# A longer hold on the first weights and x rows loaded by SyncE: a fused attention and gated-MLP kernel

## The chip, the cores and the metric

The kernel runs on one core of one Trainium2 chip. The time is device microseconds (us) of that core; "span" is the same execution as the profiler saw it, some 1.7 us shorter. A profile shows five engines: TensorE (PE for matmuls, PEld for weight loads), VectorE (DVE), ScalarE (ACT), GpSimd (POOL) and SyncE (SP), and the DMA queues: q1 is fed by SyncE, q10 by ScalarE, q0 by GpSimd. "L302" is line 302 of the kernel.

## The reference

```python
# x: 2048 x 640; wq: 640 x 6144; wo: 6144 x 640; 32 heads of 192, the last 512 cached keys and values
xn = layernorm(x)
q  = xn @ wq                                        # 32 heads
p  = softmax(q @ k[-512:].T * 192 ** -0.5)          # per head
s  = concat(p @ v[-512:]) @ wo
g  = silu((sigmoid(xn @ w_gate) * (xn @ w_up)) @ w_down)
return x + s * g
```

All inputs and the output are bf16.

## The kernel before

It starts with the gated MLP (stage B) and then does attention in 8 groups of 4 heads; each group has 4 units of 512 queries, so `NG = 8`, `NB = 4` and 32 units. The parts that matter:

The start. VectorE fills a corner of the first gate weights with zeros. Nothing needs the zeros: ScalarE's load of these weights writes over them, so it must wait for the fill, and this holds the load back by a chosen time.

```python
nc.vector.memset(wg_sb[:, 0, 0:2 * P], 0.0)       # P = 128; the hold
load_x(0, 1)                                      # SyncE: x tile 0, 160 KB
load_x(1, 1)                                      # SyncE: x tile 1
load_f(nc.scalar, wg_sb, wg_r, 0, 4, 0, 3)        # ScalarE: first gate weights, 384 KB
load_f(nc.sync, wg_sb, wg_r, 0, 4, 3, NCD)        # SyncE: the other chunks of them, 256 KB
load_f(nc.sync, wu_sb, wu_r, 0, 4, 0, 3)
load_x(2, 1)
# ... more weights and x on SyncE ...
dummy(17)                                         # matmuls on zeros while the data come
# ... statistics and centring of x tiles 0 and 1 ...
turn_pe(0, 0, 1)                                  # transposes of x tile 0 on TensorE
turn_pe(0, 1, 3, 2)
tile_half(0, 0, 0, 0, 0, 1)                       # the first real matmul, L302; needs the 384 KB
```

The end of a unit. `project` multiplies a tile of 128 queries with `wo` and adds it to `acc`; in the last group but one (`g == NG - 2`) GpSimd then applies the gate and adds the row of x, so that the last group only has to multiply, add and store.

```python
def project(u, q, k, out_eng=None, add=nc.vector, two=True):
    ...                                           # matmuls, L527
    else:
        nc.vector.tensor_tensor(cols(acc[:, t, :]), res, cols(acc[:, t, :]), ALU.add)   # L542
    if g == NG - 2:
        x_sb = fin.tile([P, D], BF16, name="row")                 # two buffers
        nc.gpsimd.dma_start(x_sb[:], xf[t * P:(t + 1) * P, :])    # L545
        nc.gpsimd.tensor_tensor(acc[:, t, :], acc[:, t, :], gate[:, t, :], ALU.mult)    # L546
        nc.gpsimd.tensor_tensor(acc[:, t, :], acc[:, t, :], x_sb[:], ALU.add)           # L547
    yield
```

In the last group VectorE multiplies the projection with the gate (L508, `o_sb`, which frees the PSUM bank) and adds `acc` (L513).

The softmax here doesn't subtract the row's maximum and nothing guards it: scores larger than these inputs give would overflow.

## Time and profile before

| | before |
|---|---|
| time, median of the 4 runs beside the changed kernel | 922.30 us (922.08 to 923.22) |
| span of the profiled run | 920.7 us |
| TensorE busy | 99% |
| first weights issued, landed, first real matmul | 1.17, 5.70, 5.74 us |
| x tile 1 landed | 4.88 us |
| GpSimd's last addition of a row ends | 885.5 us |

The prediction below shows the lines behind this table.

### The profile page before, as it was taken

The page shows a single profiled execution, that of the slowest core. Times are in us where ns is not written, and L with a number is a line of the kernel's source. Part 1 is how long each engine was busy: PE and PEld are TensorE (multiplying, and loading weights), DVE is VectorE, ACT ScalarE, POOL GpSimd, SP SyncE. Part 2 cuts the span into 40 slices and gives each one's busy share as a digit, 9 for nine tenths or more (in the row PEclk, how much of TensorE's full clock was granted, in tenths as well). Part 3 has the DMA queues.
Part 4 walks back from the last instruction along what each step waited for, and adds up shares of the span by engine and source line. Part 5 has one row for each costly group of instructions (what it writes and reads, how often), then busy time and mean ns, then how long its engine had stood idle before and what let it go on. Part 6 is the DMA issues. An engine that isn't in the chain of part 4 may idle for free.

```text
span 920.7 us, 24960 instructions
## 1 busy us (share of the span) xinstructions
PE 913.5 (99%) x11314; PEld 623.1 (68%) x11333; DVE 494.3 (54%) x987; ACT 302.9 (33%) x334; POOL 134.9 (15%) x163
## 2 busy tenths in 40 slices
PE   9999999999999999999999999999999999999998
PEld 4445455466868686867676777777776767676875
DVE  6552522544646464646555555545554646464677
ACT  4222222255142424242333333242424151515150
POOL 2000100001002000200020011001100111165733
PEclk9999999999999999999999999999999999999999
DMA  9830330125434333342425162516261615273535
GB/s 319 165 44 1 89 87 1 43 62 88 78 63 109 84 58 83 94 98 42 98 84 108 36 105 79 113 30 110 66 111 42 114 61 95 64 114 106 95 72 139
DMA packets 172106, 79.35 MB, mean 86 GB/s; under 512 B 149952, under 2 KB 167568, under 8 KB 172000
## 3 DMA queue, kind: packets, MB, share of 16 engines
q1 hardware_dynamic: 164640, 55.85, 31.5%
q0 software_dynamic: 5808, 20.52, 7.8%
q8 instruction: 88, 1.44, 0.7%
q10 hardware_dynamic: 1552, 1.39, 0.5%
q14 instruction: 18, 0.15, 0.1%
HBM read 39.45 MB, written 2.62 MB: 46 GB/s over the span
## 4 chain that ended last, share of the span: by engine, by line
PE 98%; DVE 1%; DMA 0%; issue 0%; ACT 0%; DVEq 0%
PE bank L527 22%; PE bank L456 21%; PE bank L478 19%; PE bank L438 18%; PE bank L260 8%; PE bank L272 6%; PE bank L302 3%; PE bank L404 1%; DMA wg_sb<-in_B_w_gate_dram 0%; PE bank L562 0%; DVE gate L513 0%; DVE o_sb L508 0%; ACT xnT L246 0%; PE bank L244 0%; DVEq L664 0%
## 5 line engine op out<-in xcount | busy, mean ns | idle before, releaser
L442 ACT ACTIVATE E<-bank 128x1024 bf16<-128x1024 f32 x256 | 255.3, 1022 | 457.0 <-PE bank L438 456.9
L456 PE MATMUL bank<-xnT,wq_sb 64*128 64x512 bf16 x1800 | 226.4, 376 | 0.0
L527 PE MATMUL bank<-wo_sb,oT 64*128 64x320 bf16 x2688 | 205.2, 296 | 0.0
L438 PE MATMUL bank<-qT,kT 64*128 64x512 bf16 x1536 | 200.7, 376 | 0.0
L478 PE MATMUL bank<-vbuf,E 64*128 64x193 bf16 x4096 | 195.3, 243 | 0.3 <-DVE o_sb L508 0.3
L478 PEld LDWEIGHTS <-E 64*128 64x128 bf16 x4096 | 178.8, 94 | 10.7 <-issue 1.1
L527 PEld LDWEIGHTS <-oT 64*128 64x128 bf16 (+1 forms) x2892 | 163.4, 94 | 30.6 <-issue 0.3
L463 DVE CAST qT<-bank 128x1024 bf16<-128x1024 f32 x90 | 110.2, 1225 | 128.5 <-PE bank L456 128.5
L456 PEld LDWEIGHTS <-wq_sb 64*128 64x128 bf16 x1800 | 106.2, 100 | 86.9 <-issue 0.4
L438 PEld LDWEIGHTS <-kT 64*128 64x128 bf16 x1536 | 88.2, 94 | 73.4
L491 DVE TENSOR_TENSOR o_st<-bank,rden 128x768 bf16<-128x768 f32 x128 | 122.6, 958 | 4.4
L542 DVE TENSOR_TENSOR acc<-bank,acc 128x640 f32<-128x640 f32 x96 | 79.1, 824 | 20.1 <-PE bank L527 20.1
L118 POOL DMA_DIRECT2D vbuf<-in_A_v_cache_dram x28 | 21.1, 753 | 310.5 <-PE bank L478 307.6
L461 DVE COPY seen<-bank 128x2 f32<-128x2 f32 x90 | 14.4, 160 | 79.1 <-PE bank L456 79.1
L490 DVE RECIPROCAL rden<-bank 128x4 f32<-128x4 f32 x128 | 23.4, 183 | 60.1 <-PE bank L478 59.0
L272 PE MATMUL bank<-wd_sb,hT 128*128 128x128 bf16 (+1 forms) x377 | 52.4, 298 | 0.4
L272 PEld LDWEIGHTS <-hT 128*128 128x128 bf16 x384 | 29.7, 98 | 23.1
L266 DVE TENSOR_TENSOR hT<-bank,sig 128x512 bf16<-128x512 f32 x36 | 24.8, 690 | 37.1 <-ACT sig L263 37.1
L260 PE MATMUL bank<-xnT,wu_sb 128*128 128x512 bf16 x177 | 44.6, 379 | 0.2
L260 PE MATMUL bank<-xnT,wg_sb 128*128 128x512 bf16 x176 | 44.5, 379 | 0.2
L263 ACT ACTIVATE sig<-bank 128x512 bf16<-128x512 f32 x36 | 21.5, 597 | 55.8 <-PE bank L260 52.7
L97 POOL DMA_DIRECT2D wq_sb<-in_A_wq_dram x7 | 6.3, 904 | 210.4 <-PE bank L456 210.4
(53 smaller groups left out, 408.5 us busy)
## 6 DMA issues: line engine op xcount, KB each, us to landing
wo_sb<-in_A_wo_dram SPq DMA_DIRECT2D x7, 960.0 KB, 5.6
wq_sb<-in_A_wq_dram POOLq DMA_DIRECT2D x7, 960.0 KB, 6.2
k_st<-in_A_k_cache_dram POOLq DMA_DIRECT2D x14, 384.0 KB, 5.4
vbuf<-in_A_v_cache_dram POOLq DMA_DIRECT2D x28, 192.0 KB, 3.3
row<-in_A_x_dram POOLq DMA_DIRECT2D x16, 160.0 KB, 3.1
oT<-o_st SPq DMA_TRANSPOSE x128, 3.5
x_sb<-in_A_x_dram SPq DMA_DIRECT2D x3, 640.0 KB, 9.5
wd_sb<-in_B_w_down_dram SPq DMA_DIRECT2D x1, 1920.0 KB, 13.7
```

Source lines behind the costliest of these rows:

```text
L260: nc.tensor.matmul(bank[k][:, half, 0:r1 - r0], lhsT=w[:, c, f * P:(f + 1) * P], rhs=xnT[:, b, c, r0:r1], start=(c == 0), stop=(c == NCD - 1))
L266: nc.vector.tensor_tensor(hT[b][:, f, r0:r1], bank[k][:, 1, 0:r1 - r0], sig[:, 0:r1 - r0], ALU.mult)
L272: nc.tensor.matmul(wide(k)[:, d0:d1], lhsT=hT[b][:, f, q * P:(q + 1) * P], rhs=wd_sb[:, f, d0:d1], start=(f == 0), stop=(f == NF - 1))
L302: nc.tensor.matmul(bank[k][:, half, :], lhsT=xcT[:, c, t * P:(t + 1) * P], rhs=w[:, c, fg * FT:(fg + 1) * FT], start=(c == 0), stop=(c == ...
L438: nc.tensor.matmul(bank[k][:, i, :], lhsT=kT[r, pr, j, c * P:(c + 1) * P], rhs=q[r, pr * DJ + j, :], start=(j == 0), stop=(j == DJ - 1))
L442: nc.scalar.activation(E[u, pr][:, c, :, :], bank[k][:], AF.Exp, scale=scale_qk)
L456: nc.tensor.matmul(bank[k][:, half, :], lhsT=wq[r, c, col:col + DJ * (P - 1) + 1:DJ], rhs=xnT[r, b, c, :], start=(c == 0 and not second), ...
L463: nc.vector.tensor_copy(qT[u][:, 2 * m:2 * m + 2, :], bank[k][:])
L478: nc.tensor.matmul(o4[:, q, 0:DH + 1], lhsT=e[r, c, h % 2, q * P:(q + 1) * P], rhs=vbuf[r, h, c, 0:DH + 1], start=(turn == 0 and qq == 0 a ...
L491: nc.vector.tensor_tensor(o_st[u][:, :, h * DH:(h + 1) * DH], o4[:, :, 0:DH], rden[:].to_broadcast([P, TQ, DH]), ALU.mult)
L527: nc.tensor.matmul(res[:, half, :], lhsT=oT[u][r, cc, q * P:(q + 1) * P], rhs=wo[r, cc, half * HD:(half + 1) * HD], start=(turn == 0 and c ...
L542: nc.vector.tensor_tensor(cols(acc[:, t, :]), res, cols(acc[:, t, :]), ALU.add)
```

## The change

Two intentions: to hold the first weights a little longer, so that x tile 1 passes ahead of them; and to take the row loads, with their issue and their wait, off GpSimd, and issue them before the projection that they belong to.

```diff
-        nc.vector.memset(wg_sb[:, 0, 0:2 * P], 0.0)
+        nc.vector.memset(wg_sb[:, 0:2, 0:3 * P], 0.0)
...
         res = bank[k][:, :, 0:HD]
+        if g == NG - 2:
+            x_sb = fin.tile([P, D], BF16, name="row")
+            nc.sync.dma_start(x_sb[:], xf[t * P:(t + 1) * P, :])
         for turn in range(2 if two else 1):
...
         if g == NG - 2:
-            x_sb = fin.tile([P, D], BF16, name="row")
-            nc.gpsimd.dma_start(x_sb[:], xf[t * P:(t + 1) * P, :])
             nc.gpsimd.tensor_tensor(acc[:, t, :], acc[:, t, :], gate[:, t, :], ALU.mult)
```

## The prediction

> **What bounds the kernel now.** I read the page first: busy shares, then the chain that ended last.
>
> ```profile
> PE 913.5 (99%) x11314; PEld 623.1 (68%) x11333; DVE 494.3 (54%) x987; ACT 302.9 (33%) x334; POOL 134.9 (15%) x163
> ...
> PE 98%; DVE 1%; DMA 0%; issue 0%; ACT 0%; DVEq 0%
> ```
>
> TensorE is 99% busy of a span of 920.7 us, and 98% of the chain that ended last is its matmuls; the granted clock stands in the top tenth in all 40 slices. A change that removes no matmul can win only the holes in TensorE's row. I looked for them as distances between matmul starts over 0.5 us: there are four in the whole run, before 5.74, 11.25, 14.01 and 882.88 us. The diff touches the first and the last. The first is in the chain of waits of the first 8 us (start, duration, what):
>
> ```profile
> 1.00 0.15 DVE wg_sb L172
> 1.15 0.02 issue
> 1.17 4.53 DMA wg_sb<-in_B_w_gate_dram
> 5.70 0.04 issue
> 5.74 0.38 PE bank L302
> ```
>
> The zero fill of the first gate weights (L172) releases the weights' load on ScalarE's queue; this 384 KB load lands 4.53 us after its issue, and the first real matmul follows at once. From there to the end TensorE's order is fixed and nearly gapless, so whatever moves this landing moves the end by as much. The last hole is in the chain around 880 us:
>
> ```profile
> 878.35 0.83 PE bank L527 x12
> ...
> 879.21 0.83 DVE o_sb L508
> ...
> 880.13 1.96 DVE gate L513
> 882.09 0.75 DVE o_sb L508
> 882.84 0.04 issue
> 882.88 0.84 PE bank L478 x16
> ```
>
> The matmul at 882.88 needs a PSUM bank that VectorE had still to empty (L508); VectorE was late because its addition L513 took 1.96 us where the same form takes 0.82 elsewhere. The matmuls on both sides of this hole start 0.666 us apart, against some 0.2 for an ordinary step: it costs about 0.45 us. What held VectorE is in GpSimd's timeline of that moment:
>
> ```profile
> 877.27 0.58 POOL L545 DMA_DIRECT2D row<-in_A_x_dram  x1
> 877.86 1.41 POOL L546 TENSOR_TENSOR acc<-acc,gate 128x640 f32<-128x640 f32 x1
> 880.02 1.39 POOL L547 TENSOR_TENSOR acc<-acc,row 128x640 f32<-128x640 f32 x1 [0.75 <-DMA row<-in_A_x_dram]
> 881.36 0.58 POOL L545 DMA_DIRECT2D row<-in_A_x_dram  x1
> ```
>
> GpSimd's addition of the x row runs from 880.02 to 881.41, over the start of VectorE's L513. The work belongs to group 6's tiles, whose projection ended near 870: GpSimd is more than 10 us behind, because it issues each row's load itself and then waits for it. The tile view of the row gives that price:
>
> ```profile
> L545 POOL DMA_DIRECT2D row<-in_A_x_dram x16: 549/577/590, 764.5 to 881.4; - x16
> L547 POOL TENSOR_TENSOR acc<-acc,row x16: 1390/1392/1394, 804.3 to 884.1; 128x640 f32<-128x640 f32 x16
> ...
>   DMA row<-in_A_x_dram: 19.7, 14
> ```
>
> **What the Trainium skill says.** "SBUF — State Buffer", section "Who interferes with whom": a VectorE operation with two SBUF inputs contends with a GpSimd operation that reads SBUF, and the second to start blocks until the first is done. L513 (o_sb plus acc, both in SBUF) beside L547 is this pair, and the trace agrees: 1.96 and 2.05 us in the two collisions against 0.82, each lasting until just after GpSimd's end. L508 and L542 read PSUM and one SBUF tile and keep their 0.82 us beside GpSimd work. "DMA: Bandwidth & Descriptors", section "Issuing engines are not separate DMA queues": another issuing engine saves only sequencer time. The trace agrees in part: an issue costs GpSimd 0.577 us and SyncE 0.33 to 0.45. "VectorE: DVE Perf Modes", section "Zero memsets can be issued as uint32": one cycle per element, bf16 zeros as half as many words. The trace shows 256 bf16 columns as 128 uint32 in 165 ns.
>
> **The change, part by part.**
>
> (1) Zero fill. 256 columns become 2 x 384 = 768, so 384 words for 128. Two fills in the trace (one word 60 ns, 128 words 165 ns) give 0.83 ns a word; the page's cycle at 0.96 GHz gives 1.04. Estimate: 256 more words, 0.21 to 0.27 us, and the weights' issue at about 1.40 for 1.17. VectorE itself next works at 3.04 and ScalarE at 4.21 after its table load, so only the landing counts. The DMA packets show why one would want it: nearly all of x tile 1 (issued 1.18) has moved by 3.45, but its last 3 of 128 packets go at 4.23 to 4.42, after the weights' packets began at 3.01; tile 1 lands at 4.88. With later weights these stragglers should go first and tile 1 land some half microsecond sooner. But TensorE never waits for tile 1: its transposes at 6.50 follow the matmul before them without a hole. And the weights? Most of their packets are through by 4.7; the tail to 5.28 seems to be the engine that was late with x. That engine has the same bytes to move either way, so the landing should shift by less than the delay. I take +0.05 us, between -0.2 and +0.27.
>
> (2) Row loads. GpSimd loses 16 issues of 0.577 us (9.2 us) and most of 19.7 us of waiting; SyncE gains 16 issues of about 0.4 us. Nothing of this is on TensorE's path but the collisions, so I worked through SyncE's order in the second pass over group 6 (845 to 868 us). There are two row buffers, so a load waits for the addition two tiles earlier; a GpSimd tile is 1.47 + 1.41 = 2.88 us, just under the 2.96 us at which TensorE delivers tiles (1.33 values plus 1.63 projection). Rows 0 to 3 go ahead of the four transposes issued from 857.77; these take some 1.3 us each, so row 4 is issued at about 863.0 and lands 2.3 to 2.7 us later (2.29 was the first x tile's time), near 865.5. Its addition starts then, and the seven operations from it through the last addition, back to back, end near 875.5, for 885.5 before. That is before the 880.13 collision, which goes: -0.45 us. But VectorE's first L513, at 874.28, met an idle GpSimd before and would now meet the last addition or the multiplication before it. Its slack: the bank it delays by way of the next L508 is ready at 875.85 and wanted at 876.71, 0.86 us. A block of up to 1.4 us at a phase I cannot fix costs 0 to 0.6 us; I take 0.2.
>
> Sum: 922.26 + 0.05 - 0.45 + 0.2 = about **922.05 us**, so 0.02% faster.
>
> **The rivals.**
> - SyncE becomes the wait. Head of line: in the first pass the rows stand behind eight key transposes (798.27 to 810.2), and the output transposes then stand behind rows that wait for GpSimd. My walk puts those of unit 26 7 us later, those of unit 27 12 us later and those of unit 29 1 us later. For: they were ready to go at 810.25, 822.37 and 869.40. Against: they are wanted at about 846, 857 and 896. It would need another 10 us.
> - The last values load, in GpSimd's order behind the row work, moves. It is issued at 839.30 and lands at 842.46; TensorE wants it at 845.22. I get an issue near 837, so more slack. Were rows to land 5 us late each time, it would become the bound and cost several us. Unlikely.
> - The weights land later by the whole delay, 0.27 us, or fall behind SyncE's next load of 256 KB, 0.75 us at the 340 GB/s seen there. The issue stays ahead of that one (1.40 against 1.65). Time: 922.3, or 922.8 in the worst case.
> - The transfers are hidden anyway and the collision only moves: 922.2 to 922.5.
> - Both parts win: weights land sooner for the missing contention and no collision is left: 921.6.
>
> **Range and chances.** All paths lie within 1.5 us of 922; 2% would be 18 us. The runs before spread over 0.25 us. I give 921.5 to 922.6. Faster by over 2% has 0.5%, slower by over 2% 0.5% (a wait on SyncE that I overlooked), the rest is the same.
>
> **What would show it.** In the profile after: no POOL L545; the zero fill at 0.37 to 0.44 us; x tile 1's statistics starting near 4.5 instead of 4.91; the first L302 matmul between 5.6 and 6.0. GpSimd's last L547 should end between 874 and 879 instead of 885.5. VectorE's eight full-width L513 should hold at most two long ones, among the first two, and none at 880; the 0.29 us of TensorE waiting for o_sb should be gone or sit before 877 to 878. The waits of L547 for the row should fall from 19.7 us to under 10. The prediction is wrong if TensorE shows a new wait on oT or vbuf (SyncE's order), if the first matmul starts after 6.1 (the weights lost more than their delay), or if GpSimd still works at 880.

## More of the kernel before

One more reading of the kernel before is needed for the comparison: TensorE's timeline just after the start. Its columns are start, duration, engine, line, operation, output and inputs, shapes and count.

```profile
7.41 1.25 PE L302 MATMUL bank<-wg_sb,xnT 128*128 128x512 bf16 x5
8.50 1.89 PE L302 MATMUL bank<-wu_sb,xnT 128*128 128x512 bf16 x8
```

Five matmuls of 512 columns begin at 7.41 and the next group at 8.50, so one takes 0.22 us (1.09 / 5). The duration of a group says less, because matmuls overlap.

## The result, and the profile after

| | before | after |
|---|---|---|
| time, median of 4 runs | 922.30 us (922.08 to 923.22) | 925.47 us (924.66 to 926.54) |
| span of the profiled run | 920.7 us | 924.8 us |
| first weights issued, landed | 1.17, 5.70 us | 1.44, 7.77 us |
| x tile 1 landed | 4.88 us | 3.58 us |
| GpSimd's last addition of a row ends | 885.5 us | 881.5 us |

The ratio is 1.0033 (95% interval 1.0016 to 1.0051): 0.3% slower, small but clear of noise, where 0.02% faster was predicted. Ratios here are the mean time of one kernel's fast runs over that of the other's of the same rounds, so not quite the ratio of the medians. The profiled run of the changed kernel is the slowest of its four, so its parts below add up to 4.1 us and not to the 3.2 us between the medians.

**The start.** The chain that ended last in the changed kernel, in order of time (start, duration, what):

```profile
1.02 0.39 DVE wg_sb L172
1.42 0.02 issue
1.44 6.34 DMA wg_sb<-in_B_w_gate_dram
7.77 0.04 issue
7.81 0.58 PE bank L302
```

The fill takes 0.39 us, as predicted, and the load goes out at 1.44. But the load now takes 6.34 us for 4.53, and the first real matmul starts at 7.81: 2.07 us later, for 0.27 us of hold. And the matmuls that follow are slow. The changed kernel's timeline of TensorE, the groups that answer to the two shown of before (and the first one, for the wait in brackets):

```profile
7.81 0.58 PE L302 MATMUL bank<-wg_sb,xnT 128*128 128x512 bf16 x1 [2.61 <-DMA wg_sb<-in_B_w_gate_dram]
...
10.64 2.34 PE L302 MATMUL bank<-wg_sb,xnT 128*128 128x512 bf16 x5
12.78 2.22 PE L302 MATMUL bank<-wu_sb,xnT 128*128 128x512 bf16 x8
```

Five matmuls now take 2.14 us, 0.43 us each: half speed. It lasts until about 13.4 us. It is no fall from full speed, though: the dummy matmuls on zeros, of 256 columns, start 0.213 us apart up to 4.2 us at least in every profile of this case, and at full speed such a step is 0.109 us (experiment 3). TensorE starts at half speed in every kernel; full speed had come before 5.74 us in the kernel before, and here it comes only at 13.4. From the first matmul to the one after TensorE's first wait for ScalarE (11.25 before, 15.86 after) pass 8.05 us instead of 5.51: 2.54 us more.

**Who shares the DMA engines.** The DMA view of a stretch counts packets by queue. These are the kernel before, 3.5 to 4.25 us, and the changed kernel, 4.0 to 5.0 us, each a stretch in which the first weights (q10) are on their way; the columns are packets, MB and share of the 16 engines' time:

```profile
q10 hardware_dynamic: 241, 0.24, 101.0%
q1 hardware_dynamic: 3, 0.00, 3.0%
```

```profile
q10 hardware_dynamic: 188, 0.19, 58.5%
q1 hardware_dynamic: 132, 0.14, 39.8%
```

Before, the engines do almost nothing but the first weights. After, two fifths of their time goes to SyncE's queue, and x tile 1 has long landed (3.58): these packets are SyncE's next load, the 256 KB issued at 1.65. The load is not only shared but starts slowly: from 3.0 to 4.0 us the packet records show about 66 KB of it moved, where the kernel before moved 228 KB in that time.

**The end.** Here the change does what it was meant to. GpSimd's row additions and the row loads in the changed kernel (tile view; the line numbers have moved by one to three):

```profile
L524 SPq DMA_DIRECT2D row<-in_A_x_dram x16: 327/352/1112, 814.6 to 875.4; - x16
L548 POOL TENSOR_TENSOR acc<-acc,row x16: 1398/1400/1864, 817.2 to 879.6; 128x640 f32<-128x640 f32 x16
...
  DMA row<-in_A_x_dram: 13.7, 3
```

VectorE's four additions of the stretch in which one took 1.96 us before, in the changed kernel:

```profile
878.89 1.35 DVE L513 TENSOR_TENSOR gate<-o_sb,acc 128x640 bf16<-128x640 f32 x1
...
881.09 1.10 DVE L513 TENSOR_TENSOR gate<-o_sb,acc 128x640 bf16<-128x640 f32 x1
...
884.74 0.83 DVE L513 TENSOR_TENSOR gate<-o_sb,acc 128x640 bf16<-128x640 f32 x1
...
886.78 0.83 DVE L513 TENSOR_TENSOR gate<-o_sb,acc 128x640 bf16<-128x640 f32 x1 [0.47 <-DVE o_sb L508]
```

The first two still meet GpSimd, but wait for 0.5 and 0.3 us only; the third does not meet it, and the chain passes from 883 to 888 us without VectorE. From the first matmul of L260 (33.45 us before, 38.06 after) to the end the changed kernel takes 886.71 us instead of 887.23: 0.52 us less.

The account of the profiled runs: +2.07 (later landing) +2.54 (half speed) -0.52 (rows) = +4.09, for a measured 4.10. The middle term is not the same in every execution: between the same two matmuls the other two profiles in which TensorE waited for 1.99 us or more, with no dummy matmuls added, took 6.76 us (experiment 1) and 6.97 us (768 words), so it was 1.25 and 1.46 us there.

### The profile page after: what moved, and what is told of

It reads as the page before. It is cut to its first block, busy times and chain, and to the rows that moved or that the text cites. A ratio compares the mean times of both kernels' runs of the same rounds, so it can differ in the third digit from the quotient of the medians.

```text
span 924.8 us, 24974 instructions
## 1 busy us (share of the span) xinstructions
PE 916.0 (99%) x11314; PEld 623.8 (67%) x11333; DVE 492.8 (53%) x987; ACT 303.1 (33%) x334; POOL 126.7 (14%) x147
## 3 DMA queue, kind: packets, MB, share of 16 engines
q8 instruction: 88, 1.44, 0.7%
## 4 chain that ended last, share of the span: by engine, by line
PE 98%; DMA 1%; DVE 0%; issue 0%; ACT 0%; DVEq 0%
PE bank L530 22%; PE bank L456 21%; PE bank L478 18%; PE bank L438 18%; PE bank L260 8%; PE bank L272 6%; PE bank L302 3%; PE bank L404 1%; DMA wg_sb<-in_B_w_gate_dram 1%; PE bank L563 0%; DVE o_sb L508 0%; DVE gate L513 0%; PE bank L244 0%; ACT xnT L246 0%; DVE wg_sb L172 0%
## 5 line engine op out<-in xcount | busy, mean ns | idle before, releaser
L478 PEld LDWEIGHTS <-E 64*128 64x128 bf16 x4096 | 178.8, 94 | 10.2 <-issue 0.3
L260 PE MATMUL bank<-xnT,wu_sb 128*128 128x512 bf16 x177 | 44.6, 379 | 0.2
L260 PE MATMUL bank<-xnT,wg_sb 128*128 128x512 bf16 x176 | 44.5, 379 | 0.2
L110 POOL COPY k_perm<-k_st 128x768 bf16<-128x768 bf16 x32 | 25.6, 828 | 76.1 <-DMA k_st<-in_A_k_cache_dram 76.1
```

What stands on the lines that cost most here:

```text
L110: nc.gpsimd.tensor_copy(kp[:, pr, :, :, i * H2:(i + 1) * H2], kst[:, i, :, :].rearrange("p c (i j) -> p c j i", j=DJ),)
L260: nc.tensor.matmul(bank[k][:, half, 0:r1 - r0], lhsT=w[:, c, f * P:(f + 1) * P], rhs=xnT[:, b, c, r0:r1], start=(c == 0), stop=(c == NCD - 1))
L478: nc.tensor.matmul(o4[:, q, 0:DH + 1], lhsT=e[r, c, h % 2, q * P:(q + 1) * P], rhs=vbuf[r, h, c, 0:DH + 1], start=(turn == 0 and qq == 0 a ...
```

## The experiments

All twelve kernels gave correct results. Diffs are against the changed kernel unless said otherwise. "First matmul" is the first real one (L302), from the profiled execution; times are medians.

**1. The fill alone** (the kernel before with the new fill).

```diff
-        nc.vector.memset(wg_sb[:, 0, 0:2 * P], 0.0)
+        nc.vector.memset(wg_sb[:, 0:2, 0:3 * P], 0.0)
```

> The kernel before with the wide zero fill alone. Theory START (all of the loss is the later first weights and what follows from it): 925 to 927 us, first weights landed near 7.8 us after the start, first L302 matmul at 7.8, matmuls of 512 columns at 0.43 us instead of 0.22 until about 13; and the 0.45 us hole near 880 is there again, so some 0.4 us slower than the changed kernel. Rival ROWS (the loss is on SyncE's queue): 922.3 us and weights at 5.7.

Measured: 925.23 us (923.62 to 925.76), ratio 1.0028 (1.0015 to 1.0042); weights landed at 7.12, first matmul at 7.16, 0.43 us per matmul until about 10.2. The fill is the whole loss; ROWS falls. One part of the expectation missed: the hole near 880 came back smaller (TensorE's starts 0.331 and 0.285 us apart instead of 0.666), since with the start shifted GpSimd and VectorE met at another phase.

**2. The rows alone.**

```diff
-        nc.vector.memset(wg_sb[:, 0:2, 0:3 * P], 0.0)
+        nc.vector.memset(wg_sb[:, 0, 0:2 * P], 0.0)
```

> The changed kernel with the old, narrow fill. Theory START: 921.8 us (922.3 less the 0.45 us hole at 880, which goes), weights landed at 5.7, GpSimd's last addition of a row ending near 877.5. Rival ROWS: 925 us.

Measured: 921.88 us (921.79 to 922.17, 5 runs) against 922.39 (9 runs), ratio 0.9995 (0.9982 to 1.0009): as expected in size, not resolved from zero by the times alone. The profile shows where it comes from. VectorE's first and third of the additions in question:

```profile
874.27 1.06 DVE L513 TENSOR_TENSOR gate<-o_sb,acc 128x640 bf16<-128x640 f32 x1
...
880.12 0.82 DVE L513 TENSOR_TENSOR gate<-o_sb,acc 128x640 bf16<-128x640 f32 x1
```

GpSimd's last row addition ends at 878.52, the addition at 880.12 takes its plain 0.82 us, and no two matmul starts after 210 us are over 0.25 us apart. The weights landed at 5.61. So the two parts are separate, with opposite signs.

**3. TensorE kept busy while it waits.**

```diff
         turn_pe(0, 1, 3, 2)
+        dummy(24)
         tile_half(0, 0, 0, 0, 0, 1)
```

> The changed kernel with 24 more dummy matmuls (some 2.6 us) between the first transposes and the first real matmul, so that TensorE is not idle while it waits for the weights. Theory COLD (of the 4.6 us that the start lost, 2.07 are the later landing and 2.5 are matmuls at half speed after 2.6 us of idleness): matmuls of 512 columns at 0.22 us from the first on, and 925.5 less 2.5 = about 923.0 us. Rival (the slow matmuls come from slow feeding by DMA or from other waits): they stay slow, 925.5 us.

Measured: 925.35 us, no better than the changed kernel. Yet the real matmuls were fast, 0.22 us from the first on: the first five of the added dummies still stepped at half speed (0.21 us), and from 6.0 us on they stepped at 0.109, so full speed came while TensorE was kept busy. The run was badly sized: the weights landed at 6.75, and the last dummy matmul began only at 7.99, so they cost what they saved (first matmul 8.10). Its profile also has a hole of 0.8 us at 210 us, marked "issue", which no other kernel but the other one with more matmuls (below, 0.2 us) showed; its cause was not looked for. By its time alone this run would have refuted COLD; by its matmul steps it supports it.

**4. The same with 15 dummy matmuls.**

> The changed kernel with 15 more dummy matmuls instead of 24 before the first real one; they should end near 6.9 us, about when the first weights land (6.75 to 7.77 in the runs so far), where the 24 ended at 8.2 and so took all that they gave. Theory COLD: matmuls at 0.22 us per 512 columns from the first on, first real matmul at 7.0 to 7.8, time 921.8 plus (7.0 to 7.8 less 5.7) = 923.1 to 923.9 us, some 2 us better than the changed kernel. Rival (the half speed comes from something other than idleness): still 925.5 us.

Measured: 923.86 us (923.62 to 924.89). In the profiled execution the weights landed at 8.26, later than in any other, and still:

```profile
8.30 0.38 PE L302 MATMUL bank<-wg_sb,xnT 128*128 128x512 bf16 x1 [1.50 <-DMA wg_sb<-in_B_w_gate_dram]
...
13.81 1.25 PE L302 MATMUL bank<-wg_sb,xnT 128*128 128x512 bf16 x5 [0.15 <-ACT xnT L246]
```

From 8.30 to 13.81 are 5.51 us, exactly what the kernel before takes from 5.74 to 11.25; the changed kernel took 8.05. The span is 923.1 us with a landing at 8.26, against 924.8 with one at 7.77. So the 2.54 us do not come from slow data: the rival falls. For COLD itself this profile says less than it seems to, because full speed had come before the added dummies began (they step at 0.109 us from 5.00 on). That idleness keeps TensorE at half speed rests on experiment 3, where full speed came during the dummies, and on the times of this one, whose median lies 1.6 us below the changed kernel's.

**5. SyncE's next load held back.** The changed kernel with three more fills, over the destination of that load.

```diff
         nc.vector.memset(wg_sb[:, 0:2, 0:3 * P], 0.0)
+        for _ in range(3):
+            nc.vector.memset(wg_sb[:, 3:NCD, 0:4 * P], 0.0)
```

> The changed kernel, but SyncE's next load (256 KB, the other chunks of the same weights) is held by three more zero fills over its destination until about 2.8 us, so that the first weights have the DMA engines to themselves after x tile 1. Theory SHARE (the later issue lets SyncE's next load run beside the first weights, which then get half of the packets): first weights land at 5.2 to 5.9, no cold stretch, 921.5 to 922.5 us. Rival LATE (the weights' own issue at 1.44 in place of 1.17 makes them slow, whoever else is there): they land at 7 or later again, 925 us.

Measured: 922.79 us. The first weights, issued at 1.44 as in the changed kernel, landed at 5.67, with no packet of q1 beside them between 3.75 and 4.75; DMA view of that stretch:

```profile
q10 hardware_dynamic: 279, 0.28, 83.8%
```

That decides for SHARE: the same issue time gives 5.67 us with the engines to itself and 6.75 to 8.26 in the four profiles with SyncE's load beside it. The time was 0.3 us over the expected range because SyncE was held until 3.29 us, and the up weights behind it were now late; TensorE's timeline names them:

```profile
8.94 0.81 PE L304 MATMUL bank<-wu_sb,xnT 128*128 128x512 bf16 x3 [0.31 <-DMA wu_sb<-in_B_w_up_dram]
10.12 1.24 PE L304 MATMUL bank<-wu_sb,xnT 128*128 128x512 bf16 x5 [0.37 <-DMA wu_sb<-in_B_w_up_dram]
```

The two holes cost 1.0 us (starts 0.689 and 0.751 us apart instead of 0.22).

**6. Held back by less.** One more fill instead of three.

> The changed kernel with one more zero fill (512 words, about 0.45 us) over the destination of SyncE's next load, so that this load is issued near 1.95 us instead of 1.65, after ScalarE has finished issuing the first weights (1.44 to 1.89). Theory ORDER (the first weights keep the DMA engines to themselves when their issue is over before SyncE's next one begins, as in the kernel before, 1.17 to 1.62 against 1.65): they land by 6.0 us, TensorE stays at full speed, 921.6 to 922.3 us. Rival SHARE WITHOUT ORDER (only a long lead of the first weights helps, such as the 1.8 us of the run with three fills): they land at 6.7 or later with SyncE's packets between theirs, 924 us or more.

Measured: 923.63 us (922.77 to 924.29), ratio 1.0015 (1.0000 to 1.0030). SyncE's load went out at 1.97, after ScalarE's issue had ended, and the weights landed at 6.51. ORDER falls: it does not suffice that one issue is over before the other begins. The packet records show the bulk of the weights through by 4.75 and a thin tail of some 6 KB per quarter microsecond until 6.0, beside 75 to 85 KB of SyncE's.

**7 to 11. How long a hold?** The fill alone was varied; the same kernel otherwise. The five edits, one for each run, are shown together.

```diff
-        nc.vector.memset(wg_sb[:, 0:2, 0:3 * P], 0.0)       # 384 words
+                                                            # f0: no fill
+        nc.vector.memset(wg_sb[:, 0, 0:3 * P], 0.0)         # f192
+        nc.vector.memset(wg_sb[:, 0, 0:4 * P], 0.0)         # f256
+        nc.vector.memset(wg_sb[:, 0:2, 0:320], 0.0)         # f320
+        nc.vector.memset(wg_sb[:, 0:3, 0:4 * P], 0.0)       # f768
```

> The changed kernel with a fill of 192 words (384 columns of one chunk), the first weights' issue at about 1.23 us, ending at 1.68, so 0.03 us into SyncE's next issue. Theory ORDER with a sharp edge: the weights land near 6.5 to 7.5 us in some executions, median between 922 and 925 and wide runs. Rival GRADUAL (landing moves with the issue): 5.8 us, 921.95 us.

> The changed kernel with a fill of 256 words (512 columns of one chunk), issue of the first weights at about 1.29 us, ending at 1.74, 0.09 us into SyncE's next issue. Theory ORDER: landing at 6.7 or later, 924 to 925 us. Rival GRADUAL: 5.85 us, 922.0 us.

> The changed kernel with a fill of 320 words, issue of the first weights at about 1.37 us, half way between the fill of 256 words (issue 1.30, landed 5.38, 921.8 us) and that of 384 (issue 1.44, landed 6.75 to 7.77, 925.5 us). Theory SHARE with an edge: either side, with wide runs; landing between 5.5 and 7.2, 921.9 to 925. Rival GRADUAL (landing grows with the issue by the same amount): 5.45 us, 921.9 us.

> The changed kernel without the zero fill, so that the first weights are issued at about 1.0 us, ahead of x tile 1. Theory: their packets then run against x tile 1 on SyncE's queue: weights landed by 5.0, x tile 1 at 5 or later, and the first real matmul within 0.5 us of 5.7. If the fill held nothing that matters: x tile 1 lands at 4.8 as in the kernel before.

> The changed kernel with a fill of 768 words, issue of the first weights at about 1.75 us, after SyncE's next load has begun to be issued (1.65). Theory SHARE: packets of both sides by side from the start, landing at 7.0 to 8.0, 925 to 926.5 us, not much worse than 384 words because the share and not the delay costs the time. Rival LATE (each 0.1 us of delay costs 0.5 to 1 us beyond the edge): landing at 9 or later, 928 us.

Each landing is of one profile. The runs were spread over two chips; in each group of runs the kernel before took 922.16 to 922.39 us.

| fill, words | weights issued | landed | x tile 1 landed | time, us |
|---|---|---|---|---|
| none | 0.72 | 4.56 | 5.03 | 922.59 (1 run) |
| 128 (experiment 2) | 1.17 | 5.61 | 4.80 | 921.88 |
| 192 | 1.24 | 5.09 | 3.54 | 921.98 (921.65 to 924.09) |
| 256 | 1.30 | 5.38 | 3.93 | 921.81 (921.62 to 921.91) |
| 320 | 1.37 | 6.76 | 3.55 | 922.77 (922.38 to 923.00) |
| 384 (the change) | 1.44 | 7.77 | 3.58 | 925.47 (924.66 to 926.54) |
| 768 | 1.84 | 8.04 | 3.94 | 925.76 (1 run) |

GRADUAL falls: between 1.30 and 1.37 us the landing jumps by 1.4 us. ORDER falls a second time: at 256 words ScalarE's issue overlaps SyncE's by 0.09 us and nothing happens (in that run q10 had 95.5% of the engines' time from 3.5 to 4.25 us, q1 4.9%). Past the edge the delay itself hardly counts, as SHARE has it: 0.4 us more hold (768 words) lands 0.3 us later, which is within the 6.75 to 8.26 that 384 words gave in four profiles. Without a fill the weights land early, but x tile 0 only at 3.47 instead of 3.0 to 3.1, the first real matmul waits for the transposed x (5.78), and x tile 1 waits behind the weights. That may be what the hold in the kernel before was for; the one run without it cannot say.

The length of TensorE's wait does not by itself set its speed. At 320 words TensorE was idle for 1.69 us and then ran at full speed; at 384 words it was idle for 2.61 and ran at half. But at 192 words and without a fill it idled for under 0.2 us before the first real matmul, and the first microsecond of matmuls was at half speed all the same: full speed came only at 6.6 and 7.0 us there. And at 768 words, after the longest wait, the first real matmul ran at full speed, and half speed set in later, at 8.8 us by the distances between starts, and lasted until 12.2:

```profile
8.09 0.38 PE L302 MATMUL bank<-wg_sb,xnT 128*128 128x512 bf16 x1 [2.91 <-DMA wg_sb<-in_B_w_gate_dram]
...
10.28 2.19 PE L302 MATMUL bank<-wg_sb,xnT 128*128 128x512 bf16 x5
12.31 1.89 PE L302 MATMUL bank<-wu_sb,xnT 128*128 128x512 bf16 x8
```

So the moment at which TensorE changes its speed differs between executions that began alike, and what a wait costs by half speed depends on where it meets that moment: 1.25 to 2.54 us in the three profiles with a wait of 1.99 us or more and no added dummies, 0.5 to 0.6 at 192 words and without a fill, under 0.1 in the others. The 2.54 of the changed kernel's profile, its slowest run, is in part bad luck. Half speed is also a reason why 192 words, with an earlier landing, are no faster than 256 in the profiles (spans of 920.4 and 920.1 us); the run of 924.09 us was not profiled.

The hold with 256 words is the intent of the change carried out: x tile 1 lands at 3.93 instead of 4.88 and the weights no later than before. Its median, 921.81 us, is the lowest of all kernels (in the same rounds the kernel before had 922.16), and it beats the changed kernel by 3.7 us, but the ratio to the kernel before, 0.9995 (0.9980 to 1.0010), does not prove it faster. The first matmul came at 5.42, 0.23 us sooner than in experiment 2, yet the spans are equal, 920.1 us. The chain near 876 us shows who took it back:

```profile
873.96 1.88 DVE gate L513
875.84 0.75 DVE o_sb L508
876.58 0.04 issue
876.63 0.99 PE bank L530 x12
```

VectorE's first addition met GpSimd's multiplication of a row here (873.75 to 875.15) and held a bank: matmul starts 0.434 us apart for 0.22, so 0.2 us. The prediction's rival, that the collision only moves, is real; at which phase the two meet differs from kernel to kernel.

**12. One queue for all.** No fill, and the first weights third on SyncE's queue.

```diff
-        nc.vector.memset(wg_sb[:, 0:2, 0:3 * P], 0.0)
-        load_f(nc.scalar, wg_sb, wg_r, 0, 4, 0, 3)
+        load_f(nc.sync, wg_sb, wg_r, 0, 4, 0, 3)
```

> The changed kernel without any fill and with the first weights third on SyncE's own queue (after x tiles 0 and 1), so that one queue holds all loads in order. Theory ORDER/SHARE: no packets of another load between them, so they land between 5.0 and 5.6 us, x tile 1 near 3.6, no cold stretch, 921.5 to 921.9 us. Rival (a queue of ScalarE's own is needed for the speed, as the second queue adds packets in flight): they land at 6 or later, 922.5 us or more.

Measured: 922.33 us (922.06 to 924.21). The weights were issued at 1.66, later than in the changed kernel, and landed at 5.79, two microseconds sooner; x tile 1 at 3.47; TensorE at full speed in the profile. The direction is that of SHARE, the size is missed by 0.2 to 0.8 us: this load, too, started slowly (10, 40, 63 and 68 KB in the quarters of a microsecond from 3.25), so the slow start is not a matter of two queues.

**What stays open.** Why the landing jumps just there, between an issue at 1.30 and 1.37. Shown is that a load of the same issue time is fast without SyncE's load beside it, that past the edge both queues' packets are served side by side, and that the last part of the weights comes in a thin tail while SyncE's queue fills the engines. The records do not tell which of the 16 engines moved a packet, so whether one late engine makes the tail was not shown. Nor was the slow start explained; experiment 5 had it too (some 104 KB from 3.0 to 4.0 us, with none of SyncE's load yet moving) and still landed at 5.67. What sets the moment at which TensorE reaches full speed was not varied.

## Why the prediction was wrong

The time was predicted at 922.05 us, between 921.5 and 922.6, and came out at 925.47. By the prediction's own steps:

- **The bound, and where the holes are.** Right in that TensorE's row decides. But that "whatever moves this landing moves the end by as much" did not hold: 2.07 us of landing cost 4.6 us of the profiled run before the rows gave 0.5 back (see the missing term).
- **Part 1, the fill's duration.** Right: 0.21 to 0.27 us more predicted, 0.21 measured (378 ns for 165).
- **Part 1, x tile 1.** Right, and more than predicted: it landed at 3.58 instead of 4.88, "some half microsecond" was expected. TensorE indeed gained nothing by it.
- **Part 1, the weights. This is the step that failed.** The prediction said that "the landing should shift by less than the delay", and took +0.05 us, because the late engine had the same bytes to move either way. It counted x tile 1 and the weights as the only traffic. The load that SyncE issues at 1.65 was left out of this count, though it stands in the list of rivals in a milder form, as a load that the weights could fall behind, at a cost of 0.75 us. In the runs it ran beside them: the term measured +2.07 us, and without SyncE's load it all but vanished (5.67 us in experiment 5).
- **A term that was missing.** The sum had no price for TensorE sitting idle. It named a first matmul after 6.1 us as the sign of failure, but took such a delay for a shift and nothing more. In the profiled run TensorE, which had not yet reached full speed, idled for 2.61 us and then ran the next 5.6 us at half speed: 2.54 us, more than the delay itself, and 1.25 and 1.46 us in the other two profiles of that kind. With dummy matmuls in the wait the term is gone (experiments 3 and 4), though only experiment 3 saw full speed come during them.
- **Part 2, the collision.** Right in kind, and better than predicted: "- 0.45 + 0.2", so 0.25 us net, was expected, and 0.52 us was measured from the first matmul of L260 to the end, in the changed kernel and in experiment 2, because the 0.2 for a new collision did not come there. One reading of the lines was loose: the two long additions end 0.68 us after GpSimd's, most of an addition later, and not just after. Against experiment 1, where the old row loads met VectorE at a kinder phase, the same stretch is only 0.2 us shorter (886.71 for 886.91). The walk through SyncE's order put GpSimd's end at about 875.5; experiment 2 has 878.52 (877.4 and 877.1 with other fills). The collision at 874 that was feared costs up to 0.2 us, in one of the profiles, as the prediction's second number had it.
- **The rivals on SyncE's side.** None came. No wait on the transposed outputs or the values appears in the chain; the transposes of unit 27 were issued from 835.0 in the changed kernel, 12.6 us later than before, of which 4.6 are the later start, and in time.

## What to carry to other kernels

A hold that lets one transfer go first is a position in a queue of several: before lengthening it, list every load that is issued between the old release and the new landing, because the delayed one may come to share the engines with them, and vary the hold in small steps, since here the step from 256 to 320 words, 0.07 us of hold, cost 1.4 us of landing and 1.0 us of time. Price a delay at the head of a kernel with what the waiting engine loses by idling as well, and read a start-to-start distance of matmuls to see it. And judge a change of two parts by each part alone: the useful 0.5 us was here hidden under a loss that was 4.6 us in the profiled run.

## What the Trainium skill lacked or had wrong

- "TensorE: Matmul & The Clock Gate", section "Part 1: The HAM clock gate (the "warmup" mystery)", says that what is issued in the first 3.4 us or so runs at half clock and everything after at full clock. As a budget this is too short: in experiment 3 TensorE worked nearly without a pause from 1.05 us and reached full speed at 6.0, after 5.0 us; in the changed kernel, with a wait, at 13.4. The window of about 3.4 us that the same section describes, which runs freely, fits both: the half speed at 768 words lasted 3.4 us (8.8 to 12.2). An estimate from the page's 3.413 us: counted back from 13.45, the windows of the changed kernel's profile end at 10.04, 6.63 and 3.22, and TensorE worked through none of them. The page does not say how busy a window must be. By the same count 2.2 us of work (7.81 to 10.04) were too few in the changed kernel, and 3.0 us (7.16 to 10.2) sufficed in experiment 1. The speeds agree with the page: its 427 and 216 ns per 512 columns are 0.43 and 0.22 us here. The granted clock of the profile's page stayed in its top tenth in all 40 slices and did not show the half speed.
- "DMA: Bandwidth & Descriptors", section "Queues, rings and completion order", says that an engine takes turns between the queues it has work for, packet by packet. The changed kernel agrees (188 and 132 packets in 1 us). The kernel before does not obviously: SyncE's load had been issued 1.85 us earlier, and 3 of 244 packets between 3.5 and 4.25 us were from its queue. Beyond a first-byte latency the page has nothing on when an issued load's packets get their turn, and so nothing on the jump of 1.4 us for 0.07 us of hold.
- "VectorE: DVE Perf Modes", section "Zero memsets can be issued as uint32 (trn2)", gives one cycle per element: 256 more words would be 0.27 us at the 0.96 GHz of the same page (an estimate). Measured: 378 less 165 ns, 0.21 us, so 0.83 ns per word. A page that used a fill as a delay would need this number.
